# An attention, dense and routed-expert kernel: turns of the searches, halves for two copies, a bank for two logit tiles, and a number moved

## The chip, the cores and the metric

The kernel runs on one core of a Trainium2 chip. The metric is the device time of one execution in microseconds (us); the time of a kernel is the median of its runs. TensorE (PE) multiplies matrices, VectorE (DVE), ScalarE (ACT) and GpSimd (POOL) work on elements, SyncE (SP) and the others issue transfers (DMA). PSUM is the memory, in banks of 512 fp32 columns, into which PE writes; SBUF is the working memory.

## What is computed

Three stages follow each other: a linear attention with random features, a dense two-layer network, and eight experts to which 2304 tokens are assigned greedily, at most 288 tokens each, by order of their logits. The last stage, in which the change lies:

```python
logits = x @ w_gate                      # x: 2304 x 512, eight experts
order = np.argsort(-logits.flatten())
for idx in order:
    tok, e = idx // E, idx % E
    if assigned[tok] >= 0 or counts[e] >= cap:
        continue
    assigned[tok] = e
    counts[e] += 1
for e in range(E):
    h = np.maximum(x[assigned == e] @ w1[e], 0.0)
    out[assigned == e] = h @ w2[e]
```

## The kernel before

**Stages.** Attention runs to about 195 us, the dense network to about 609 us, the experts to the end. Products are made as three matmuls each (`mm3`, lines 203 to 206), of a high and a low part of both operands.

**The end of the dense network.** It works on five blocks: four of four tiles of 128 tokens, and one of the two tiles 16 and 17. `st_B` (L581) adds up the second layer in PSUM accumulators (tag `pj`). `st_x` (L546) copies each finished accumulator to SBUF (`xs`, L548), sends the rows to `xd` in DRAM (L550; tile 17 from ACT's queue, all others from SP's), and either notes eight dot products for DVE (`st_dot`, L562) or, for the tiles in `LT`, notes the tile for products on PE: `st_lT` (L565) transposes it (L569) and copies the transpose to SBUF (`xTt`, L571), `st_lg` (L574) multiplies it with the gate (L578) into the single bank of tag `tp` and reads eight logits out (L579). For tiles 16 and 17 this happens at the very end, in L641 to L643.

**The searches.** `finds` (L739) runs eight searches, numbered 0 to 7. Each finds the next expert that fills up, and its tokens. `begin` (L668) sets up keys from the logits `lg`. `closest` (L701) narrows a threshold in six iterations: DVE compares (`cmp`, L698), PE counts (L714), DVE tests (`ge`, L716), PE spreads the result (L719), DVE moves on (`dk` L723, `v2` L726). Then DVE marks the members (`so` L751, `sel` L754, `mem` L756 and L757), with `whose` (L786: L789, L791) writing the expert's number `e` between `so` and `sel`; PE counts places (`slots`, L800 and L801), and `numbers` (L811: `aa` L815 to L818, one-hots `OH` L832, their product L836) gives the token indices `idx` (L841). `outm` (L760) marks the tokens that stay. For searches 0, 1, 6 and 7 the numbers are finished in the search itself (yield `OH`); for 2 to 5 in the first two iterations of the following search (`fill`).

**The order of the work.** PE runs in the written order; the other engines' order is set by a planner from priorities and estimated readiness. Search 0 runs alone. When its indices are there, `fetch_x` (L855) gathers the expert's rows on POOL (L860), and a DVE instruction (L866) that waits for the last gather holds back the rest of the weights' loads on SP (`fetch_w`, L845). Meanwhile one step of search 1, and then `N1` more, go out (L989 to L991); then come the transposes of the gathered rows (`prep`, L879), and then the experts (`mlp`, L891). `mlp` gives control back after each turn of products, that is after one `mm3` of three matmuls, 64 times per expert; `visit` (L979) counts these turns down and takes the next step of the searches when `wait` runs out. How many turns lie between two steps is in `GAP` (L45), by the name of the step that the search has just yielded. So long as fewer than two searches are finished, L985 caps it at 3. From turn 57 of an expert on, the next expert's rows are transposed.

Of the kernel before, what the change touches and what calls it, by code (L numbers as in the profile page):

```python
# [20 lines left out]
def fused(tc, q, k, v, omega, w_in, w_out, w_gate, w1, w2, out):  # L21
# [22 lines left out]
    FZ, FS, PZ, PS = 6, 2, 56, 2  # L44
    HPF, RP, N1, GAP = 400, 30, 4, dict(cmp0=12, cmp5=3, cmp6=4, ge=2, mem=6, OH=7)  # L45
    DM = H * D
# [5 lines left out]
    with ctx:  # L52
# [493 lines left out]
        def st_x(t, acc):  # L546
            x = mb.tile([P, DM], F32, tag="xs", name="xs", bufs=XS)
            (nc.vector.tensor_copy if t % 2 and not 12 <= t < 16 else nc.scalar.copy)(x, acc)  # L548
            for rows, dst in x_rows(t):
                (nc.scalar if t == 17 else nc.sync).dma_start(dst, x[rows])  # L550
            if t in LT:
                xrow.append((t, x))
            else:

                dots.extend((acc if t >= 14 else x, lg[:, t, e:e + 1], e) for e in range(8))
# [3 lines left out]
        def st_dot(n):  # L559
# [3 lines left out]
            del dots[:n]  # L563

        def st_lT(x, copy):  # L565

            pt = ps("big")
            for c in range(4):
                nc.tensor.transpose(pt[:, c * P:(c + 1) * P], x[:, c * P:(c + 1) * P], ident)  # L569
            xT = mp.tile([P, DM], F32, tag="junk", name="xTt", bufs=2)  # L570
            copy(xT, pt)  # L571
            return xT

        def st_lg(t, xT):  # L574

            pg = ps("tp")
            for c in range(4):
                nc.tensor.matmul(pg[:, :8], xT[:, c * P:(c + 1) * P], wgn[:, c], start=c == 0, stop=c == 3, skip_group_check=True)  # L578
            nc.vector.tensor_scalar(lg[:, t], pg[:, :8], 0.0, None, ALU.add)  # L579

# [23 lines left out]
        def step(i):  # L604
# [28 lines left out]
            if i < len(steps):  # L633
                if t is not None:
                    st_lg(t, xT)
                st_dot(ND if i <= NB * NF else NE)
            elif i + 1 - LB == len(steps):
                st_dot(len(dots))
                nc.vector.tensor_scalar(lg[:, 0:12], lg[:, 0:12], 0.0, None, ALU.add)
                nc.vector.tensor_scalar(lg[:, 14:16], lg[:, 14:16], 0.0, None, ALU.add)  # L640
                xTs = [st_lT(x, copy) for (t, x), copy in zip(xrow, (nc.scalar.copy, nc.vector.tensor_copy))]  # L641
                for (t, x), xT in zip(xrow, xTs):
                    st_lg(t, xT)  # L643

# [94 lines left out]
        def finds():  # L739
# [3 lines left out]
            for k in range(E):  # L743
                res = rs[k]
                if k < E - 1:
# [5 lines left out]
                    nc.vector.tensor_tensor(so, st[0], e1b, ALU.mult)  # L751
                    whose(res, e1)
                    sel = small("sel", (P, NT))
                    nc.vector.tensor_reduce(sel, so, AX.X, ALU.max)  # L754
                    mem = small("mem", (P, 2, NT), BF)
                    nc.vector.scalar_tensor_tensor(mem[:, 0], vf, 0.0, sel, ALU.is_gt, ALU.mult)  # L756
                    nc.vector.scalar_tensor_tensor(mem[:, 1], vf, 0.0, sel, ALU.is_equal, ALU.mult)  # L757
                    q_ = yield from slots(mem.rearrange("p a t -> p (a t)"), 2)
                    out_ = small("outm", (P, NT))
                    nc.vector.tensor_scalar(out_, q_, GP + 0.5, None, ALU.is_gt)  # L760
                else:
# [6 lines left out]
                if k in (0, 1, E - 2, E - 1):  # L768
# [6 lines left out]
                    if k == 0:  # L775
                        yield "first"
                if k < E - 1:

                    nc.vector.scalar_tensor_tensor(lg, e1b, -3.0e38, lg, ALU.mult, ALU.add)
                    nc.vector.tensor_tensor(opn, opn, e1, ALU.subtract)  # L780

                    nc.vector.tensor_tensor(wt, wt, bc_e(out_), ALU.mult)
# [196 lines left out]
        def visit():  # L979
            wait[0] -= 1  # L980
            if wait[0] < 0:
                with tc.high_priority(offset=RP):
                    z = next(route, None)

                wait[0] = min(GAP.get(z, 0), 3) if found[0] < 2 else GAP.get(z, 0)  # L985

# [59 lines left out]
```

## Time and profile before

| | us |
|---|---|
| median of three runs (lowest to highest) | 958.03 (957.17 to 958.26) |
| the profiled execution, its own time | 955.96 |
| the profiled execution, its span from first to last instruction | 953.9 |

The span is 2.06 us shorter than the execution's own time, which is 2.07 us below the median. The mean granted TensorE clock is 0.962 of full speed. Times in rows count from the span's start. In rows of the order of time, the first two numbers are start and duration in us; `ACTq` and `SPq` are the DMA issues of an engine; a bracket at the end says how long the engine had been idle before the instruction, and what ended that.

### The profile page before, as it was taken

The numbers are of one execution on the slowest core, as the hardware profiler recorded it, in microseconds if no ns is written. First come the engines' busy times: TensorE is split into PE (matmuls) and PEld (weight loads), VectorE is DVE, ScalarE is ACT, GpSimd is POOL, SyncE is SP. The second block draws the span as 40 slices with busy tenths as digits, with TensorE's granted clock in tenths as the row PEclk, the third lists the DMA queues.
The fourth block names the chain that finished last, engine by engine and source line by source line (L and its number), as shares of the span: only waits on it lengthen the run. The fifth ranks groups of instructions, "written<-read, shape, count | busy, mean of one in ns | idle before, by whom it ended". The sixth has DMA issues, their size and how long they took to land. (4 is left out here: it accounts for less than half of the span.)

```text
span 953.9 us, 16517 instructions
## 1 busy us (share of the span) xinstructions
PE 877.3 (92%) x5923; PEld 770.3 (81%) x5923; DVE 630.1 (66%) x1645; ACT 483.9 (51%) x1062; POOL 476.3 (50%) x443
## 2 busy tenths in 40 slices
PE   7999799989999999999999999738998999998996
PEld 6998698968678888888888889628887888888996
DVE  4779889868877943882397256466774847866442
ACT  5777798955455355434534466303343343443552
POOL 6669756336664455445446446312443534436442
PEclk9999899999999999999999999858998989999999
DMA  8855532012311000100010010023641616428500
GB/s 209 222 158 168 133 111 68 23 67 67 108 70 44 1 1 1 45 0 1 1 45 1 0 45 2 23 69 133 202 165 62 203 45 208 154 74 256 197 26 25
DMA packets 74850, 81.90 MB, mean 86 GB/s; under 512 B 27016, under 2 KB 59784, under 8 KB 74640
## 3 DMA queue, kind: packets, MB, share of 16 engines
q1 hardware_dynamic: 71536, 71.15, 23.6%
q0 software_dynamic: 3072, 9.44, 3.2%
q8 instruction: 46, 0.75, 0.3%
q14 instruction: 36, 0.29, 0.1%
q10 hardware_dynamic: 160, 0.26, 0.1%
HBM read 71.39 MB, written 9.45 MB: 85 GB/s over the span
## 5 line engine op out<-in xcount | busy, mean ns | idle before, releaser
L905 POOL TENSOR_TENSOR iL<-We,iH 128x512 fp32r<-128x512 f32 x63 | 87.9, 1395 | 141.9 <-ACT iH L902 129.3
L496 POOL TENSOR_TENSOR iL<-W,iH 128x512 fp32r<-128x512 f32 x80 | 114.6, 1432 | 68.7 <-ACT iH L495 64.5
L204 PE MATMUL kv<-xH,iH 128*128 128x512 f32 (+2 forms) x372 | 130.3, 350 | 1.8 <-ACT xH L511 1.8
L206 PE MATMUL kv<-xH,iL 128*128 128x512 f32 (+2 forms) x372 | 127.7, 343 | 2.6 <-POOL iL L496 2.6
L205 PE MATMUL kv<-xL,iH 128*128 128x512 f32 (+2 forms) x372 | 127.9, 344 | 0.9 <-DVE xL L512 0.9
L504 POOL TENSOR_TENSOR oL<-W,oH 128x512 fp32r<-128x512 f32 x56 | 72.9, 1302 | 104.3 <-ACT oH L503 104.3
L206 PE MATMUL pj<-oH,gL 128*128 128x512 f32 x288 | 113.8, 395 | 0.0
L204 PE MATMUL pj<-oH,gH 128*128 128x512 f32 x288 | 113.7, 395 | 0.0
L205 PE MATMUL pj<-oL,gH 128*128 128x512 f32 x288 | 113.4, 394 | 0.0
L902 ACT CAST iH<-We 128x512 fp32r<-128x512 f32 x64 | 39.5, 619 | 113.8 <-PE kv L205 37.4
L269 ACT ACTIVATE kp<-pj,bias 128x128 f32<-128x128 f32 x288 | 79.1, 409 | 17.6 <-DVE bias L261 14.5
L562 DVE SCALAR_TENSOR_TENSOR junk<-xs,wgb 128x512 f32<-128x512 f32 x96 | 86.5, 948 | 0.0
L204 PE MATMUL pj<-hH,oH 128*128 128x288 f32 x256 | 84.1, 328 | 0.0
L206 PEld LDWEIGHTS kv<-xH,iL 128*128 128x128 f32 x372 | 71.6, 193 | 11.1 <-POOL iL L496 4.3
L204 PEld LDWEIGHTS kv<-xH,iH 128*128 128x128 f32 x372 | 71.4, 192 | 11.2 <-issue 3.0
L495 ACT CAST iH<-W 128x512 fp32r<-128x512 f32 x80 | 49.7, 621 | 59.1 <-PE kv L205 38.5
L205 PEld LDWEIGHTS kv<-xL,iH 128*128 128x128 f32 x372 | 71.6, 192 | 9.0 <-DVE xL L512 1.5
L205 PE MATMUL pj<-hL,oH 128*128 128x288 f32 x256 | 77.4, 302 | 0.6 <-DVE hL L927 0.5
L178 POOL TENSOR_TENSOR stg<-cg,stg 128x512 f32<-128x512 f32 x32 | 41.7, 1303 | 71.6 <-issue 30.4
L206 PE MATMUL pj<-hH,oL 128*128 128x288 f32 x256 | 76.9, 301 | 0.0
L532 DVE SCALAR_TENSOR_TENSOR kv<-r,kv 128x512 f32<-128x512 f32 (+1 forms) x53 | 34.0, 642 | 59.7 <-ACT r L531 59.6
L206 PE MATMUL s<-xH,iL 128*128 128x288 f32 (+2 forms) x204 | 68.6, 336 | 2.3 <-POOL iL L496 2.3
(377 smaller groups left out, 2262.0 us busy)
## 6 DMA issues: line engine op xcount, KB each, us to landing
We<-in_moe_w_dram SPq DMA_DIRECT2D x64, 512.0 KB, 4.5
stg<-in_moe_w_in_dram SPq DMA_DIRECT2D x16, 512.0 KB, 5.2
stg<-in_moe_w_out_dram SPq DMA_DIRECT2D x16, 512.0 KB, 3.5
ld<-in_k_dram SPq DMA_DIRECT2D x8, 512.0 KB
vf<-in_v_dram SPq DMA_DIRECT2D x32, 128.0 KB, 3.1
ld<-in_q_dram SPq DMA_DIRECT2D x8, 512.0 KB, 4.9
xd<-xs SPq DMA_DIRECT2D x16, 256.0 KB, 2.2
wgb<-wgd SPq DMA_DIRECT2D x1, 2048.0 KB
```

What stands on the lines that cost most here:

```text
L178: nc.gpsimd.tensor_tensor(lf, g.bitcast(F32), lf, ALU.mult)
L204: nc.tensor.matmul(o, aH, bH, start=first, stop=False, skip_group_check=True)
L205: nc.tensor.matmul(o, aH, bL, start=False, stop=False, skip_group_check=True)
L206: nc.tensor.matmul(o, aL, bH, start=False, stop=last, skip_group_check=True)
L269: nc.scalar.activation(kp[:, i, j], pjs[s // 4][:, s % 4], AF.Exp, bias=bias[:, i, j:j + 1])
L495: nc.scalar.copy(iH, wi)
L496: on_pool.append(nc.gpsimd.tensor_tensor(iL, wi, iH.bitcast(F32), ALU.subtract).ins)
L504: (nc.gpsimd if (ib > 0 if ib < NB else f % 2 == 0) else nc.vector).tensor_tensor(oL, wo, oH.bitcast(F32), ALU.subtract)
L532: nc.vector.scalar_tensor_tensor(ph[:, :n], r[:, :n], 1.0, ph[:, :n], ALU.min, ALU.mult)
L562: nc.vector.scalar_tensor_tensor(junk, x, 1.0, wgb[:, e], ALU.mult, ALU.mult, accum_out=d)
L902: nc.scalar.copy(iH, wi)
L905: (nc.vector if first and f == 0 else nc.gpsimd).tensor_tensor(iL, wi, iH.bitcast(F32), ALU.subtract)
```

## The change

- **Turns.** `N1` goes from 4 to 3; in `GAP`, `cmp5` goes from 3 to 4, `cmp6` from 4 to 5, `ge` from 2 to 1. While fewer than two searches are finished, every gap but that of `ge` is two smaller than in `GAP`, in place of the cap at 3.
- **Halves.** The accumulators of tiles 16 and 17, and their transposes, are each copied half by ACT and half by DVE (`both`).
- **One bank.** The logits of tiles 16 and 17 are made side by side in one PSUM bank and read by one instruction.
- **The number and `outm`.** `whose` stands behind the marks; `outm` stands behind the part of `numbers` that belongs to the search.

```diff
--- before.py
+++ after.py
@@ -42,7 +42,7 @@
 
     W1C, W2C, Z0 = 4, 4, 2
     FZ, FS, PZ, PS = 6, 2, 56, 2
-    HPF, RP, N1, GAP = 400, 30, 4, dict(cmp0=12, cmp5=3, cmp6=4, ge=2, mem=6, OH=7)
+    HPF, RP, N1, GAP = 400, 30, 3, dict(cmp0=12, cmp5=4, cmp6=5, ge=1, mem=6, OH=7)
     DM = H * D
     DFF = w_in.shape[1]
     N = B * S
@@ -545,7 +545,10 @@
 
         def st_x(t, acc):
             x = mb.tile([P, DM], F32, tag="xs", name="xs", bufs=XS)
-            (nc.vector.tensor_copy if t % 2 and not 12 <= t < 16 else nc.scalar.copy)(x, acc)
+            if t < 16:
+                (nc.vector.tensor_copy if t % 2 and t < 12 else nc.scalar.copy)(x, acc)
+            else:
+                both(x, acc)
             for rows, dst in x_rows(t):
                 (nc.scalar if t == 17 else nc.sync).dma_start(dst, x[rows])
             if t in LT:
@@ -561,6 +564,10 @@
                 junk = mp.tile([P, DM], F32, tag="junk", name="junk", bufs=2)
                 nc.vector.scalar_tensor_tensor(junk, x, 1.0, wgb[:, e], ALU.mult, ALU.mult, accum_out=d)
             del dots[:n]
+
+        def both(y, x):
+            nc.scalar.copy(y[:, 0:256], x[:, 0:256])
+            nc.vector.tensor_copy(y[:, 256:512], x[:, 256:512])
 
         def st_lT(x, copy):
 
@@ -571,12 +578,14 @@
             copy(xT, pt)
             return xT
 
-        def st_lg(t, xT):
+        def st_lg(t, xTs):
 
             pg = ps("tp")
-            for c in range(4):
-                nc.tensor.matmul(pg[:, :8], xT[:, c * P:(c + 1) * P], wgn[:, c], start=c == 0, stop=c == 3, skip_group_check=True)
-            nc.vector.tensor_scalar(lg[:, t], pg[:, :8], 0.0, None, ALU.add)
+            for j, xT in enumerate(xTs):
+                for c in range(4):
+                    nc.tensor.matmul(pg[:, 8 * j:8 * j + 8], xT[:, c * P:(c + 1) * P], wgn[:, c], start=c == 0, stop=c == 3,
+                                     skip_group_check=True)
+            nc.vector.tensor_scalar(lg[:, t:t + len(xTs)].rearrange("p t e -> p (t e)"), pg[:, :8 * len(xTs)], 0.0, None, ALU.add)
 
         def st_B(i):
             ib, f = steps[i]
@@ -632,15 +641,13 @@
                 st_B(i - LB)
             if i < len(steps):
                 if t is not None:
-                    st_lg(t, xT)
+                    st_lg(t, [xT])
                 st_dot(ND if i <= NB * NF else NE)
             elif i + 1 - LB == len(steps):
                 st_dot(len(dots))
                 nc.vector.tensor_scalar(lg[:, 0:12], lg[:, 0:12], 0.0, None, ALU.add)
                 nc.vector.tensor_scalar(lg[:, 14:16], lg[:, 14:16], 0.0, None, ALU.add)
-                xTs = [st_lT(x, copy) for (t, x), copy in zip(xrow, (nc.scalar.copy, nc.vector.tensor_copy))]
-                for (t, x), xT in zip(xrow, xTs):
-                    st_lg(t, xT)
+                st_lg(16, [st_lT(x, both) for t, x in xrow])
 
         i = 0
         with tc.manual_schedule(engines={ET.DVE, ET.Pool, ET.PE, ET.Activation}):
@@ -749,15 +756,13 @@
                     e1b = e1.unsqueeze(1).to_broadcast([P, NT, E])
                     so = small("so", (P, NT, E))
                     nc.vector.tensor_tensor(so, st[0], e1b, ALU.mult)
-                    whose(res, e1)
                     sel = small("sel", (P, NT))
                     nc.vector.tensor_reduce(sel, so, AX.X, ALU.max)
                     mem = small("mem", (P, 2, NT), BF)
                     nc.vector.scalar_tensor_tensor(mem[:, 0], vf, 0.0, sel, ALU.is_gt, ALU.mult)
                     nc.vector.scalar_tensor_tensor(mem[:, 1], vf, 0.0, sel, ALU.is_equal, ALU.mult)
+                    whose(res, e1)
                     q_ = yield from slots(mem.rearrange("p a t -> p (a t)"), 2)
-                    out_ = small("outm", (P, NT))
-                    nc.vector.tensor_scalar(out_, q_, GP + 0.5, None, ALU.is_gt)
                 else:
 
                     whose(res, opn)
@@ -775,6 +780,8 @@
                     if k == 0:
                         yield "first"
                 if k < E - 1:
+                    out_ = small("outm", (P, NT))
+                    nc.vector.tensor_scalar(out_, q_, GP + 0.5, None, ALU.is_gt)
 
                     nc.vector.scalar_tensor_tensor(lg, e1b, -3.0e38, lg, ALU.mult, ALU.add)
                     nc.vector.tensor_tensor(opn, opn, e1, ALU.subtract)
@@ -982,7 +989,7 @@
                 with tc.high_priority(offset=RP):
                     z = next(route, None)
 
-                wait[0] = min(GAP.get(z, 0), 3) if found[0] < 2 else GAP.get(z, 0)
+                wait[0] = GAP.get(z, 0) - 2 * (found[0] < 2 and z != "ge")
 
         with tc.manual_schedule(engines={ET.PE}):
             with tc.issue_after(rs[0]["placed"].ins):
```

## Rows read from the trace of the kernel before

**Rows 1.** The page's first part: busy us (share of the span) xinstructions, by engine
```profile
PE 877.3 (92%) x5923; PEld 770.3 (81%) x5923; DVE 630.1 (66%) x1645; ACT 483.9 (51%) x1062; POOL 476.3 (50%) x443
```

**Rows 2.** Busy time by stretch, columns named in the first line
```profile
core 0: us, PE busy (x) PEld busy (x) DVE busy (x) ACT busy (x) POOL busy (x), PEclk, DMA share, GB/s
...
615.00:620.00 5.00, 1.58 (x38) 1.31 (x38) 3.32 (x20) 0.00 (x0) 1.58 (x17) 0.50 0.01 3
...
665.00:670.00 5.00, 2.77 (x21) 2.40 (x19) 4.97 (x31) 1.55 (x3) 0.81 (x2) 1.00 0.22 63
...
770.00:775.00 5.00, 5.00 (x31) 4.65 (x28) 2.30 (x8) 1.81 (x4) 0.00 (x0) 0.50 0.00 0
775.00:780.00 5.00, 5.00 (x46) 4.64 (x45) 2.91 (x9) 2.25 (x5) 0.72 (x1) 0.87 0.01 3
...
900.00:905.00 5.00, 5.00 (x39) 5.00 (x39) 1.68 (x4) 2.68 (x6) 2.35 (x2) 1.00 0.00 0
```

**Rows 3.** Waits of PE from 647 us on: total us, times, longest
```profile
PE kv L886 <- DMA xg<-xd,idx: 4.8, 5, 1.2
...
PE tp L714 <- DVE cmp L698: 3.4, 6, 1.1
PE tp L800 <- DVE mem L757: 3.0, 3, 1.7
PE tp L719 <- DVE ge L716: 1.3, 3, 0.7
```

**Rows 4.** Order of time: tiles 16 and 17, and a half-size cast
```profile
598.80 0.37 ACT L533 CAST gH<-kv 128x256 fp32r<-128x256 f32 x1
...
608.82 0.59 ACT L548 COPY xs<-pj 128x512 f32<-128x512 f32 x1 [2.08 <-PE pj L206]
...
609.52 0.69 DVE L548 COPY xs<-pj 128x512 f32<-128x512 f32 x1 [2.33 <-PE pj L206]
...
610.25 1.24 ACTq L550 DMA_DIRECT2D xd<-xs  x2
...
612.11 1.63 PE L578 MATMUL tp<-wgn,xTt 128*128 128x8 f32 x8 [0.26 <-DVE lg L579]
...
613.98 0.17 DVE L579 TENSOR_SCALAR lg<-tp 128x8 f32<-128x8 f32 x1
```

**Rows 5.** Order of time: ACT and DVE at tile 14's accumulator
```profile
563.92 0.61 ACT L548 COPY xs<-pj 128x512 f32<-128x512 f32 x1
...
564.07 0.42 DVE L534 TENSOR_TENSOR gL<-s,gH 128x256 fp32r<-128x256 f32 x1 [0.90 <-ACT gH L533]
564.56 0.69 DVE L562 SCALAR_TENSOR_TENSOR junk<-pj,wgb 128x512 f32<-128x512 f32 x1
```

**Rows 6.** Order of time on DVE: marks of search 0
```profile
630.47 0.31 DVE L751 TENSOR_TENSOR so<-oh,e 128x144 f32<-128x144 bf16 x1
...
630.82 0.30 DVE L754 TENSOR_REDUCE sel<-so 128x18 f32<-128x144 f32 x1
...
632.43 0.18 DVE L760 TENSOR_SCALAR outm<-q__6676 128x18 f32<-128x18 f32 x1
632.52 0.17 DVE L815 TENSOR_SCALAR aa<-q__6676 128x18 f32<-128x18 f32 x1
```

**Rows 7.** Order of time on PE: the last steps ahead of the first expert
```profile
643.49 0.64 PE L714 MATMUL tp<-oh,cmp 128*32 128x8 bf16 x18 [1.76 <-DVE cmp L698]
...
644.80 0.55 PE L886 MATMUL kv<-ident,xg 96*128 96x96 f32 x2 [0.26 <-issue]
...
646.97 0.61 PE L204 MATMUL kv<-xH,iH 128*128 128x288 f32 x1
```

**Rows 8.** Order of time on PE: marks and one-hots of search 1
```profile
667.62 0.18 PE L800 MATMUL tp<-mem,ta 128*128 128x36 bf16 x1 [1.74 <-DVE mem L757]
...
670.75 1.08 PE L836 MATMUL tp<-mv,OH 128*96 128x6 bf16 x18 [1.23 <-DVE OH L832]
```

**Rows 9.** Order of time on PE: two waits of searches 2 and 3
```profile
681.42 0.61 PE L714 MATMUL tp<-oh,cmp 128*32 128x8 bf16 x18 [0.49 <-DVE cmp L698]
...
714.09 0.16 PE L719 MATMUL tp<-ge,onesu 32*128 32x8 bf16 x1 [0.68 <-DVE ge L716]
```

## The prediction

> **What bounds the kernel now.** I read the page's busy times first, then the busy time by stretch, then the waits of PE, then the instructions in order of time at the four places that the diff touches. TensorE is busy 92% of the span [rows 1], so what can be won is idle time of PE, and time at its lower clock. Both lie behind 609 us. From 615 to 620 us PE works 1.6 of 5 us, at half clock: the first search runs with nothing beside it, and DVE, PE and POOL hand a chain on until the first expert starts at 647 us [rows 2]. Behind that, PE works in its written order: expert products, and between them the small products of the next searches. One turn of products (three matmuls, after which the kernel looks whether a search step is due) takes 5.00 / 39 x 3 = 0.385 us at full clock, by the stretch 900 to 905 us [rows 2]. PE's waits behind 647 us are few and have names [rows 3]: 4.8 us on gathered rows, 3.4 us on comparisons, 3.0 us on marks, 1.3 us on `ge`, and further ones on one-hot tiles. In such a place DVE is full: 4.97 of 5 us between 665 and 670 us [rows 2]. The time of the whole is thus an entry chain of about 37 us, plus PE's work, plus these waits (12.5 us in the four rows) and what the half clock costs.
>
> **Copies in halves, logits in one bank.** Now tile 16 is copied by ACT at 608.82 us in 0.59 us, tile 17 by DVE from 609.52 to 610.21; the second group of logit products waits until DVE has emptied the bank of the first, runs 1.63 us from 612.11 (part of it at half clock), and its result is read at 613.98 [rows 4]. A half tile costs ACT 0.37 [rows 4] and DVE 0.42 us [rows 5] (a 128x256 cast and a subtraction that read PSUM, nearest in shape). If both halves run at once, tile 17 is ready at 609.95, each later copy ends 0.16 to 0.26 us sooner, the second group needs no emptied bank and runs mostly at full clock: read at about 612.85, 1.1 us won. If the halves of one bank go in turn, a copy takes 0.37 + 0.05 + 0.42 = 0.84 us, 0.25 and 0.15 us more than now. Then tile 17 is whole at 610.36, its transposes end near 611.0; ACT's queue also holds tile 17's two DMA issues, 1.24 us together [rows 4], which become ready before that transposed tile and sit ahead of its ACT half until 611.6; ACT and DVE halves end at 612.0 and 612.5, and the products at 613.0 to 613.4. That is still 0.3 to 0.7 us won, because the emptying in between is gone. If those DMA issues also come ahead of tile 16's transposed half, 0.3 us is lost. Which of the two it is, the nearest row says: DVE's first reading of tile 14's accumulator starts at 564.56 us, 0.03 us after ACT's copy of the same bank ended (563.92 + 0.61), though DVE had been free from 564.49 (564.07 + 0.42) [rows 5]: that looks like one engine at a time. I take 0.4 us won, between -0.3 and 1.1.
>
> The Trainium skill, "PSUM — Partial Sum Buffer", section "PSUM bank collisions raise a hardware error", speaks against this part: two engines on one bank and the same partitions at once, even two reads, are an error that software keeps apart by a dependency. By that rule the halves go in turn and the part is worth 0.4 us; without it, 1.1 us. The two rows agree with it, but are one case.
>
> **Expert's number behind the marks; `outm` later.** In search 0, `sel` (L754) starts at 630.82, 0.04 us after its input `so` (630.47 + 0.31) is done: the number's instruction at L789 fits into the latency in front of it [rows 6], so moving it wins nothing there. It makes `e`, and SP's load of the first expert's weights, some 0.4 us later. Nothing else is queued on SP then; the cover is the gather, for that load goes out about when L760 runs, at 632.4 [rows 6], and the first product starts only at 646.97 us [rows 7]. If that cover were gone it would cost these 0.4 us. `outm` (L760) stands in front of the `aa` of L815 by 0.09 us [rows 6]; moved behind the one-hots it runs under the gather: 0.1 us won. In later searches DVE has no gaps, and the three small instructions delay `mem` by 0 to 0.3 us; see below.
>
> **N1 from 4 to 3.** Before the first expert, PE's order holds L714, L719, L714, L719 of search 1 and then the transposes of the gathered rows. The last L714 ends at 643.49 + 0.64 = 644.13 us, the transposes start at 644.80 [rows 7]. With the last L719 moved behind the first turn of products they start about 0.6 us sooner (0.4 to 0.7: a semaphore wait may remain). Its follow-up on DVE (`dk`, `v2`, comparison) moves behind the expert's first splits, where three turns at half clock hide it. 0.6 us won, on the chain.
>
> **GAP, search 1.** I counted the turns by hand from the two formulas. The marks' product L800 comes at turn 28 (was 29), its `mem` is asked for at turn 23 (was 25), the one-hots' product L836 at 34 (was 33). So five turns instead of four lie in front of L800, which now waits 1.74 us, and six instead of four in front of L836, which waits 1.23 [rows 8]: 0.38 + 0.77 us, and 0.2 for the number's instructions, 1.35 at most. Against it, comparison 3 gets three turns instead of four, which may cost up to 0.55; and DVE, full there, may stretch. I take 0.8, between 0 and 1.4.
>
> **GAP, searches 2 to 6.** A comparison gets one turn more before its product, `ge` one less; an iteration keeps its seven or eight turns, except the first, so that a search takes 59 instead of 60. Where DVE is late, the wait only moves from L714 to L719 and nothing is won. Where only the comparison is late it is: 0.38 of the 0.49 us at 681.42 us [rows 9]. The other two waits on marks are 3.0 - 1.74 = 1.26 us together [rows 3]; with the number behind them I take 0.2 off each. Sum 0.8, between 0.2 and 1.0. The one-hots' product that frees the gather of expert 2 comes at turn 115 instead of 116, of expert 3 at 174 instead of 176, the gathered rows are wanted at 121 and 185 as before. At most 0.38 + 0.77 = 1.15 us of the 4.8 us on gathers goes; but `ge` stood late at just that place (0.68 us at 714.09 us [rows 9]) and eats about half: 0.6, between 0 and 1.1.
>
> **Sum.** 0.4 + 0.1 + 0.6 + 0.8 + 0.8 + 0.6 = 3.3 us off the profiled execution, whose span is 953.9 us and whose own time is 955.96: 950.6 and 952.7. The median of the runs shown is 958.03, 2.07 above that execution; so I forecast 954.7 for a median. The ends give 0.4 to 5.4 won, 957.6 to 952.6.
>
> **Rivals.** *A spared clock drop* (0.20): behind the wait on expert 3's rows the clock is 0.50 from 770 to 775 us and 0.87 in the next stretch [rows 2]: 5 + 1.3 us at half clock cost 3.15 us. If the shorter wait keeps the clock up, 954.7 - 3.15 = 951.5. For it: this wait shrinks most, by two turns. Against: the neighbours' waits remain, and drops may come up elsewhere. *Only the entry wins* (0.24): the searches are bound by DVE, the waits move from L714 to L719 one for one, and 0.4 + 0.1 + 0.6 = 1.1 us stays: 956.9. For it: 4.97 of 5 us on DVE. *Slower, by `ge`* (0.14): in the first two iterations of searches 2 to 6, where DVE also makes the older search's numbers, `ge` is queued behind them, and PE stands at L719, in order, with all later products behind it, one turn longer, while the comparison's extra turn pays nothing because DVE was not late there: 10 x 0.385 = 3.85 us lost, 1.1 won at the entry: 960.8. It decides once the waits at L719 grow from 1.3 to over about 3 us and those at L714 stay. Against it: only 3 waits on `ge` exist behind 647 us now.
>
> **How the numbers follow.** The forecast holds 0.42, the rivals 0.20, 0.24 and 0.14. The likeliest time is 954.7. Eight in ten reach from 951.0, just below the spared drop, to 959.5; beyond lie most of the slower case and the better ends of the spared drop. A measurement of this kernel tells about 0.2%, 1.9 us, from no change. Faster than 956.1: most of the forecast, the spared drop and a little of the entry case, 0.60. Slower than 959.9: 0.13. Between: 0.27.
>
> **What would show it.** Right: the last logit read 0.3 to 0.7 us sooner after the last product, with DVE's half behind ACT's; the first expert product about 1.1 us sooner than 646.97; L800 and L836 of search 1 waiting under 2.2 us together; L719 waits below 2.5 us. Wrong: halves that run beside each other, ACT's halves behind the DMA issues of both tiles, L719 waits above 3 us, or a clock that stays up from 770 to 780 us.

## The result and the profile after

The changed kernel takes 946.46 us (median of 7 runs, 945.88 to 947.95) where the kernel before takes 958.03; the ratio, estimated from all runs of both and not the quotient of the medians, is 0.9893, with a 95% interval from 0.9873 to 0.9912. It is faster by 11.6 us in medians and by 10.2 us by the ratio; the forecast was 3.3 us, 954.7, and the time lies below its range. In the table below, one slow run of e15 (1671 us) is left out. The profiled execution of after has a span of 943.9 us and a time of 946.46, against 953.9 and 955.96. In the changed kernel the lines from about 569 on are 7 higher: L714 is now L721 (`cmp`), L719 is L726 (`ge`), L800 is L807 (`mem`), L836 is L843 (`OH`), L886 is L893 (gathered rows).

First the page's busy times of after, against [rows 1]: the engines do nearly the same work; of PE's 2.9 us less, some 1.5 are the shorter time at half clock, below.

```profile
PE 874.4 (93%) x5923; PEld 768.3 (81%) x5923; DVE 634.6 (67%) x1646; ACT 485.0 (51%) x1064; POOL 475.2 (50%) x443
```

Then PE's waits of after from 646 us on (total us, times, longest), against [rows 3]:

```profile
PE tp L726 <- DVE ge L723: 2.4, 5, 0.6
PE kv L893 <- DMA xg<-xd,idx: 2.4, 3, 0.9
PE pj L205 <- DVE hL L934: 1.7, 2, 0.9
PE tp L721 <- DVE cmp L705: 1.4, 3, 0.8
PE tp L721 <- DVE oh L694: 1.1, 2, 0.6
PE tp L843 <- DVE dk L730: 1.0, 4, 0.3
PE tp L807 <- DVE mem L763: 1.0, 3, 0.6
PE tp L843 <- DVE OH L839: 0.5, 1, 0.5
```

Three lines of before that [rows 3] leaves out:

```profile
PE tp L836 <- DVE OH L832: 4.2, 3, 2.1
...
PE tp L714 <- DVE oh L687: 0.6, 1, 0.6
PE pj L205 <- DVE hL L927: 0.5, 1, 0.5
```

Gathered rows are down from 4.8 to 2.4 us, `cmp` from 3.4 to 1.4, `mem` from 3.0 to 1.0, the one-hots from 4.2 to 0.5; `ge` is up from 1.3 to 2.4, `hL` from 0.5 to 1.7, `oh` from 0.6 to 1.1. Next the entry in order of time, against [rows 4] and [rows 7]:

```profile
608.89 0.37 ACT L569 COPY xs<-pj 128x256 f32<-128x256 f32 x1 [2.08 <-PE pj L206]
609.30 0.42 DVE L570 COPY xs<-pj 128x256 f32<-128x256 f32 x1 [2.03 <-ACT xs L569]
...
612.27 1.07 PE L586 MATMUL tp<-wgn,xTt 128*128 128x8 f32 x8 [0.53 <-ACT xTt L569]
...
613.47 0.17 DVE L588 TENSOR_SCALAR lg<-tp 128x16 f32<-128x16 f32 x1 [0.79 <-PE tp L586]
...
643.59 0.64 PE L721 MATMUL tp<-oh,cmp 128*32 128x8 bf16 x18 [2.43 <-DVE cmp L705]
644.16 1.22 PE L893 MATMUL kv<-ident,xg 96*128 96x96 f32 x6
...
646.37 0.61 PE L204 MATMUL kv<-xH,iH 128*128 128x288 f32 x1
```

The last logit is read 0.51 us sooner (613.47 against 613.98), the first expert product starts 0.60 us sooner (646.37 against 646.97). So of the 10.0 us between the two spans, 0.6 come from the entry, and 9.4 from the stretch between the first expert product and the last transposes of results, which shrinks from 298.5 to 289.1 us.

I took that stretch apart in the same way for every run below: **length** from the first expert product to the end of the last transposes, **idle**, the sum of the gaps between PE's instructions in it, **rows**, the part of idle in front of the transposes of gathered rows, and **half clock**, the time in it in which the granted clock was 0.5 of full speed, the lower of its two levels (a stretch with a clock between counts by its share; by 0.5 us windows of busy time). Half clock costs half its length. Before: 298.5, idle 19.2, half clock 23.5. After: 289.1, 11.5, 20.6. So 7.7 of the 9.4 us are waits and some 1.5 are clock; what is left, 0.2, shows in neither. By experts' stages (the first from the first product, the others from the first transposes of that expert's rows, each to those of the next), the gain is in the first (37.0 to 34.9 us), the fourth (43.6 to 37.6, with the waits on expert 3's rows) and the sixth (37.3 to 32.0, with the waits on the last one-hots); the third and the fifth lost 2.5 and 2.1.

### The profile page after: what moved, and what is told of

It reads as the page before. It is cut to its first block, busy times and chain, and to the rows that moved or that the text cites. A ratio compares the mean times of both kernels' runs of the same rounds, so it can differ in the third digit from the quotient of the medians.

```text
span 943.9 us, 16523 instructions
## 1 busy us (share of the span) xinstructions
PE 874.4 (93%) x5923; PEld 768.3 (81%) x5923; DVE 634.6 (67%) x1646; ACT 485.0 (51%) x1064; POOL 475.2 (50%) x443
## 5 line engine op out<-in xcount | busy, mean ns | idle before, releaser
L912 POOL TENSOR_TENSOR iL<-We,iH 128x512 fp32r<-128x512 f32 x63 | 84.2, 1339 | 133.0 <-ACT iH L909 125.4
L269 ACT ACTIVATE kp<-pj,bias 128x128 f32<-128x128 f32 x288 | 79.4, 411 | 17.9 <-DVE bias L261 14.5
```

Source lines behind the costliest of these rows:

```text
L269: nc.scalar.activation(kp[:, i, j], pjs[s // 4][:, s % 4], AF.Exp, bias=bias[:, i, j:j + 1])
L912: (nc.vector if first and f == 0 else nc.gpsimd).tensor_tensor(iL, wi, iH.bitcast(F32), ALU.subtract)
```

## The experiments

Times are medians; the ratio is that to the kernel before, run beside it on the same chip, with its 95% interval. The last four columns are of the profiled execution.

| kernel | turns a search | us | ratio | length | idle | rows | half clock |
|---|---|---|---|---|---|---|---|
| before | 60 | 958.0 | 1 | 298.5 | 19.2 | 4.8 | 23.5 |
| e9 | 61 | 959.7 | 1.0029 [1.0010, 1.0047] | 299.1 | 19.9 | 6.9 | 24.1 |
| e5 | 59 | 949.3 | 0.9921 [0.9904, 0.9937] | 291.8 | 16.2 | 2.1 | 14.4 |
| e10 | 58 | 962.1 | 1.0049 [1.0028, 1.0069] | 305.1 | 22.8 | 1.6 | 34.0 |
| e2, tail | 60 | 956.5 | 0.9996 [0.9979, 1.0014] | 300.2 | 19.5 | 4.8 | 26.5 |
| e3, marks | 60 | 956.4 | 0.9993 [0.9977, 1.0009] | 298.6 | 19.3 | 4.9 | 24.0 |
| e6, exchange | 60 | 956.2 | 0.9991 [0.9972, 1.0010] | 300.1 | 17.6 | 3.9 | 31.5 |
| e8, search 6 sooner | 60 | 954.9 | 0.9979 [0.9964, 0.9993] | 297.8 | 17.7 | 4.7 | 27.1 |
| e1, all turns | 59 | 951.1 | 0.9931 [0.9907, 0.9955] | 288.6 | 14.1 | 2.4 | 13.4 |
| e4, later turns | 59 | 952.0 | 0.9934 [0.9913, 0.9956] | 294.5 | 16.6 | 0.9 | 21.4 |
| e7, turns and marks | 59 | 949.1 | 0.9907 [0.9883, 0.9931] | 291.4 | 14.9 | 3.0 | 17.6 |
| after | 59 | 946.5 | 0.9893 [0.9873, 0.9912] | 289.1 | 11.5 | 2.4 | 20.6 |
| e11, after, search 6 later | 59 | 947.8 | 0.9901 [0.9875, 0.9928] | 291.0 | 13.2 | 2.5 | 20.6 |
| e16, after | 60 | 957.4 | 1.0010 [0.9993, 1.0027] | 299.1 | 18.0 | 5.4 | 30.9 |
| e12, after | 58 | 960.5 | 1.0038 [1.0018, 1.0058] | 301.4 | 20.2 | 1.0 | 27.4 |
| e13, before, half splits | 60 | 955.0 | 0.9967 [0.9945, 0.9989] | 297.0 | 17.6 | 5.1 | 23.0 |
| e15, e10, half splits | 58 | 951.5 | 0.9944 [0.9924, 0.9964] | 295.3 | 17.0 | 2.1 | 23.6 |
| e14, after, half splits | 59 | 944.8 | 0.9883 [0.9859, 0.9908] | 286.1 | 11.7 | 3.2 | 14.0 |
| e17, before, no splits on POOL | 60 | 940.4 | 0.9830 [0.9805, 0.9855] | 283.3 | 8.6 | 5.4 | 20.0 |
| e18, e10, no splits on POOL | 58 | 935.1 | 0.9781 [0.9758, 0.9804] | 277.1 | 5.7 | 2.0 | 12.7 |

### The parts of the change by themselves

e1 is the kernel before with the three edits of turns alone (`N1`, `GAP`, the `wait` of `visit`); e2 has `both` and the one bank alone; e3 has `whose` and `outm` moved alone; e4 has the new turns only from the third search on, with `N1` 4.

```
e4:  wait[0] = dict(cmp0=3, cmp5=3, cmp6=3, ge=2, mem=3, OH=3).get(z, 0) if found[0] < 2 else GAP.get(z, 0)
     N1, GAP = 4, dict(cmp0=12, cmp5=4, cmp6=5, ge=1, mem=6, OH=7)
```

> The kernel before with the changed turns alone (N1, GAP, the formula); copies, logits and marks as before. Theory A, the turns: they take away nearly all of the 7.7 us of PE idle time that are gone behind the first expert's first product; the entry gains under 0.4 us. Expected 949.5 us (947.5 to 951.5) where the kernel before has 958.0. Theory B, a sum of small shifts: what is gone hangs on where the searches of the last experts fall against POOL's splits, so that any part moves it; then this run lies anywhere from 950 to 957 and the parts don't add up. Theory C, the marks: the turns alone give 3 us at most, 955.

> The kernel before with the copies in halves and the logits in one bank alone. Theory A: the last logits are read 0.5 us sooner, nothing else moves: 957.5 (956.5 to 958.0), with the idle time of PE behind the first expert's first product between 18 and 20.5 us. Theory B: a shift of 0.5 us of the whole entry changes later waits by 2 us or more either way. Theory C as A.

> The kernel before with the expert's number behind the marks and outm behind the numbers alone. Theory A: 0.1 us at the entry and 0.2 us at each of three waits on marks: 957.4 (956.5 to 958.0); the last search still waits about 2 us at its one-hots' product. Theory C, the marks: DVE's chain from the marks to the one-hots is what is freed in every search; then this run alone gives 4 us or more, below 954.5, and the waits on one-hots (4.2 us) fall below 2.

> The kernel before with the new turns only from the time on when two searches are finished (cmp5 4, cmp6 5, ge 1), and N1 and all gaps of search 1 as before. Theory A in its finer form: the idle time that went lies mostly in the stretches of experts 3 and 5 (2.7 and 2.9 of 7.7 us), so this run keeps about 6 us of the gain: 952 (950.5 to 954). If search 1's turns matter more (its waits fell by 1.2 us, and the clock came back 3.2 us sooner), it keeps 4 us or less: above 954.

The turns win 5.8 us by themselves (951.09 against 956.87 of the kernel before, run beside it; the profiled execution of e1, 945.21, was its fastest, so its last four columns flatter it). Tail and marks by themselves are not told apart from no change. By the ratios the three parts add up to 0.80%, the whole change to 1.07%; the intervals are too wide to say whether the parts help each other. With `N1` and search 1's turns as before (e4) it is 951.99: these two are worth less than the runs tell apart, though each shows in the trace (below; the later searches of e4 also stand one turn sooner than those of e1, for search 1 is a turn shorter there). What can be measured of the gain is in the turns of the searches from the third on.

### Which property of the turns

The new numbers do two things: they give `cmp` a turn more and `ge` a turn less, and they make a search 59 turns long instead of 60. e5 has only the second, e6 only the first. Counted in the traces, the searches of e5 stand one turn sooner than those of the changed kernel (its one-hots' products come at turns 114, 173 and 232, against 115, 174 and 233 there and 116, 176 and 236 before), since search 1 is as before in it. e7 is the change without its tail. e8 is the kernel before with its last search alone four turns sooner.

```
e5:  GAP = dict(cmp0=11, cmp5=3, cmp6=4, ge=2, mem=6, OH=7)                          (before: cmp0=12)
e6:  e4's two lines with cmp0=13
e8:  wait[0] = min(GAP.get(z, 0), 3) if found[0] < 2 else GAP.get(z, 0)
    +wait[0] -= 4 * (z == "cmp0" and found[0] == 5)
```

> The kernel before with one number changed: cmp0 from 12 to 11, so that each search from the third on takes 59 turns instead of 60, as in the changed kernel, while cmp5, cmp6 and ge keep their old turns. Theory D, the drift: what wins is that later searches, and with them the gathers of experts 2 and 3 and the one-hots of the last two searches, come one to four turns sooner against the experts' products. Then this run keeps what the late turns alone kept: 952 (950.5 to 953.5), with no wait on expert 3's rows above 1 us and less than 0.5 us on the last one-hots. Theory E, the exchange: what wins is the comparison's extra turn at the price of ge's; then this run stays at 956 to 958.

> The kernel before with the new turns of cmp5, cmp6 and ge from the time on when two searches are finished, and cmp0 raised from 12 to 13, so that a search keeps its 60 turns: the exchange without the drift. Theory D: 956 to 958.5, with waits on expert 3's rows (1.7 us) and on the last one-hots (2 us or more) as before. Theory E: 952 (950.5 to 953.5).

> The changed kernel with the copies and logits of tiles 16 and 17 as before: turns and marks together. The turns alone took 951.1 and the changed kernel 946.5. If turns and marks help each other (the changed kernel waits 0.55 us on ge at search 5's first iteration where the turns alone wait 1.83 us), this run is near the changed kernel: 947.2 (946 to 948.5). If it is the copies that move the entry against the clock's fall, it stays near 951.

> The kernel before with search 6 alone begun four turns sooner, so that searches 6 and 7 stand at the turns that the changed kernel gives them, and all else as before. Theory D: the waits on the last two one-hots (0.9 and 2.1 us) fall under 0.5 us together and the half-clock stretch behind them goes: 3 to 4.5 us faster, 953 (951.5 to 954.5). If the place against the products doesn't matter: 956 to 958, with those waits still there.

One number, `cmp0` 11 for 12, wins 7.8 us; the exchange of `cmp` and `ge` wins nothing that can be measured. That one turn adds up from search to search: in the changed kernel the one-hots' product for expert 3's rows comes two turns sooner, the last one four. Of the 6.7 us that e5's length loses, 2.6 are waits on rows and some 4.5 half clock, which is 9.1 us shorter; the other waits are 14.1 us against 14.5, for the two on the last one-hots are gone and others have come. Two lines of e5's waits:

```profile
PE kv L886 <- DMA xg<-xd,idx: 2.1, 2, 1.1
...
PE tp L836 <- DVE OH L832: 1.2, 1, 1.2
```

e7 lies between its two cases, and its interval overlaps those of e1 and of after: it decides nothing. e8 takes the two waits on the last one-hots away (the sixth stage goes from 37.3 to 31.7 us, idle 0.06), but a wait of 1.85 us comes up at 830 us, on the one-hots `oh` with which the last search starts, and 2.2 us are left of the gain:

```profile
829.22 1.49 POOL L905 TENSOR_TENSOR iL<-We,iH 128x512 fp32r<-128x512 f32 x1 [1.66 <-ACT iH L902]
...
829.49 1.38 DVE L676 TENSOR_TENSOR w__9811<-w__9811,ta 128x144 f32<-128x144 f32 x1
...
832.02 0.62 PE L714 MATMUL tp<-oh,cmp 128*32 128x8 bf16 x18 [1.85 <-DVE oh L687]
```

L676 makes an input of `oh` and takes 0.3 us elsewhere; I saw what stands beside it only later (below).

After these I held that a search that stands sooner has more margin: rows and one-hots come before PE wants them. The next four were to show that.

### The margin holds for the rows alone

```
e9:  cmp0=13, e10: cmp0=10            (in the kernel before)
e12: cmp0=11                          (in the changed kernel; 58 turns there)
e11: +wait[0] += 4 * (z == "cmp0" and found[0] == 5)      (in the changed kernel)
```

> The kernel before with one turn more between two searches (cmp0 13: a search takes 61 turns, not 60). Theory of the margin (a search that is k turns later against the products lets PE wait k turns longer for gathered rows and for the last one-hots, and the clock falls behind such waits): the waits on expert 2's and 3's rows and on the last one-hots, which are there already, grow by 1 to 6 turns of 0.385 us each, idle time of PE from the first product on rises from 18 to 21 us or more, and the time is 3 to 6 us above that of the kernel before. Rival (the gain of 59 turns was a lucky place of a few waits and clock drops): within 2 us of the kernel before, idle time 17 to 19 us.

> The kernel before with two turns less between two searches (cmp0 10: 58 turns). With 59 turns it gained 7.8 us. Theory of the margin: the waits on rows and last one-hots are gone already with 59, so a further turn wins at most 1 to 2 us and may lose as much on comparisons, since each search stands closer behind the numbers of the one before: 947 to 952. Rival (every turn sooner counts the same): 941 to 943.

> The changed kernel with its last search alone held back by four turns, so that its one-hots come where they came before. Theory of the margin: two waits on the last one-hots near 865 and 872 us come back, 2 to 3 us together, and a stretch of half clock behind them: 948.5 to 951, with the last stages as in the kernel before. Rival (the stage before expert 7's rows is won by another part of the change): no wait there, within 1 us of the changed kernel's 946.5.

> The changed kernel with one turn less between two searches (cmp0 11: 58 turns, not 59). Theory of the margin: the changed kernel still waits 2.4 us on gathered rows and 1.1 us on oh in three to five places; a turn sooner takes 0.4 to 1 us of these, and comparisons may eat it: 945 to 948. Rival (each turn sooner wins some 7 us as it did in the kernel before): 939 to 941.

For the gathered rows the theory holds: their waits are 6.9, 4.8, 2.1 and 1.6 us with 61, 60, 59 and 58 turns, and 2.4 and 1.0 in the changed kernel with 59 and 58. For the whole it falls. A turn more than 60 costs 2.7 us, less than expected, since the waits on the last one-hots shrink to 0.09 and 0.67; and a turn less than 59 loses 12.8 us in the kernel before (949.3 to 962.1) and 14.0 in the changed one (946.5 to 960.5). With 58 turns the searches are sooner everywhere, and yet the waits on the last one-hots are back, longer than with 60 (2.69 and 1.02 us in e10), and there are others on `cmp`, `ge` and `oh`, of 2.4, 1.7 and 1.7 us. The rival that each turn sooner wins as much again falls too. e11 has one of the two waits back, 2.2 us at 865 us, and half clock behind it; its 1.3 us over the changed kernel are less than the two intervals tell apart.

What these waits have in common shows in the order of time on DVE and POOL. The kernel before, ahead of its last one-hots:

```profile
869.76 1.85 DVE L815 TENSOR_SCALAR aa<-sl 128x18 f32<-128x18 f32 x1
870.28 1.29 POOL L905 TENSOR_TENSOR iL<-We,iH 128x512 fp32r<-128x512 f32 x1
...
871.86 1.45 POOL L905 TENSOR_TENSOR iL<-We,iH 128x512 fp32r<-128x512 f32 x1 [0.29 <-ACT iH L902]
...
872.11 1.27 DVE L822 TENSOR_TENSOR jj<-aa 128x54 f32<-128x54 f32 x1
...
874.26 1.08 PE L836 MATMUL tp<-mv,OH 128*96 128x6 bf16 x18 [2.06 <-DVE OH L832]
```

L815 takes 0.17 us elsewhere [rows 6]; here it takes 1.85 and ends at 871.61, 0.04 us behind POOL's split of the expert's weights (870.28 + 1.29). L822, 0.22 us elsewhere, is held by the next split likewise. These two holds, 2.7 us together, cover what PE waits, 2.06 us. The same place in the changed kernel:

```profile
861.37 0.18 DVE L822 TENSOR_SCALAR aa<-sl 128x18 f32<-128x18 f32 x1
...
862.57 1.12 DVE L839 TENSOR_TENSOR OH<-tb,q 128x864 bf16<-128x864 bf16 x2
...
863.61 3.21 DVE L916 TENSOR_TENSOR oL<-We,oH 128x256 fp32r<-128x256 f32 x1
863.99 2.53 POOL L912 TENSOR_TENSOR iL<-We,iH 128x512 fp32r<-128x512 f32 x2
864.00 0.93 PE L843 MATMUL tp<-mv,OH 128*96 128x6 bf16 x18
```

Here the search's steps run while POOL issues gathers, and the one-hots' product goes without a wait; the hold falls on `oL`, a split for a product that comes later. With 58 turns (e10) the hold is on the one-hots themselves:

```profile
876.05 2.19 DVE L832 TENSOR_TENSOR OH<-tb,q 128x864 bf16<-128x864 bf16 x2
876.09 1.68 POOL L905 TENSOR_TENSOR iL<-We,iH 128x512 fp32r<-128x512 f32 x1 [1.15 <-ACT iH L902]
876.71 0.56 PE L836 MATMUL tp<-mv,OH 128*96 128x6 bf16 x9 [2.69 <-DVE OH L832]
```

Over the whole stretch I compared each DVE instruction with the lower quartile of its own line, tile and shape. In the kernel before, 18 last over 0.8 us longer than that, in the changed kernel 19, and each of them lies beside one of POOL's splits; instructions that lie beside none sum to 2 to 3 us of excess. The sum beside splits is not what differs (22.2 us before, 26.7 after), and its part on steps of the searches differs little (20.6 before, 19.4 after): which step is hit, with how much slack, sets the wait. That is a theory so far; it predicts that shorter holds, with all turns left alone, bring 58 turns back.

### Shorter holds, and none

In e13 to e15 POOL's split is cut in two; the order of the instructions of PE and ACT stays the same to the last one in the traces, and so does that of DVE but for swaps of neighbours in a few places of e13 and e14. e16 is the changed kernel with 60 turns. In e17 and e18 the splits on POOL are left out, a tile of zeros stands for their results, and PE makes the same products in the same order (some neighbours on DVE change places).

```
e13, e14, e15:
-   (nc.vector if first and f == 0 else nc.gpsimd).tensor_tensor(iL, wi, iH.bitcast(F32), ALU.subtract)
+   for c in [slice(0, 4)] if first and f == 0 else [slice(z, z + 2) for z in range(0, 4, 2)]: (nc.vector if first and f == 0 else nc.gpsimd).tensor_tensor(iL[:, c], wi[:, c], iH[:, c].bitcast(F32), ALU.subtract)
e16: cmp0=13 in the changed kernel
e17, e18:
+   zL = rp.tile([P, 4, P], F32R, tag="zL", name="zL", bufs=1)              (once, ahead of the experts)
+   nc.gpsimd.memset(zL.bitcast(F32), 0.0)
...
-   iL = rp.tile([P, 4, P], F32R, tag="iL", name="iL", bufs=2)
+   iL = rp.tile([P, 4, P], F32R, tag="iL", name="iL", bufs=1) if first and f == 0 else zL
...
-   (nc.vector if first and f == 0 else nc.gpsimd).tensor_tensor(iL, wi, iH.bitcast(F32), ALU.subtract)
+   if first and f == 0:
+       nc.vector.tensor_tensor(iL, wi, iH.bitcast(F32), ALU.subtract)
```

> The kernel before, with the splits of the weights that POOL makes (iL, 128x512 in about 1.3 us) cut into two instructions of 128x256; the order of all engines is otherwise as before, to the last instruction, and so are the turns. Theory of the collisions (a DVE instruction of a search that falls beside one of POOL's splits is held until that split ends; which one is hit decides the waits): a hit holds 0.65 us instead of 1.3 to 1.85, the two waits on the last one-hots (0.90 and 2.06 us) fall below 1.5 us together, idle time of PE behind the first product falls from 18 to 15 us, and the time to 951 to 955. Rival (what counts is the turn at which a step is asked for): the turns are the same, so 956 to 958, with the same waits.

> The changed kernel with POOL's splits in halves likewise. Theory of the collisions: its hits fall mostly on oL, which has slack, so little is left: 944 to 946.5. Rival (turns): 946 to 947.5. If shorter splits slow POOL down as a whole: above 948.

> The kernel before with 58 turns a search, which took 962.1 us and waited 2.7, 2.4 and 1.7 us in places where it waited little with 60, and with POOL's splits in halves. Theory of the collisions: those long waits fall to about half, 953 to 958. Rival (58 turns are too few for the comparisons by themselves): 960 to 963.

> The changed kernel with one turn more between two searches, so that a search takes 60 turns as before, while all its other parts stay (halves, one bank, marks, N1, the turns of search 1, cmp and ge exchanged). If the place of the later searches against the experts carries the gain: 952 to 956, with other waits and clock drops in the stages of experts 2 to 5. If the other parts carry it: 947 to 949.

> The kernel before without POOL's splits of the experts' first weights: the low parts iL are left out (one constant tile of zeros stands for them), all products are still made, so that PE has the same work in the same turns (60 a search) and POOL keeps only its gathers and scatters. Theory of the collisions: no DVE instruction is held by over 0.8 us, waits on the one-hots of the last search (0.90 and 2.06 us) go below 0.7, idle time behind the first product from 18 to 10 to 14 us; 943 to 951. Rival (the waits come from the turns and from DVE's load alone): waits as before, 954 to 958.

> The same (POOL's low parts left out) with 58 turns a search, which with the splits cost 5 us over 60 turns. Theory of the collisions: without them 58 and 60 turns stand within 3 us of each other, both under 951. Rival (58 turns are too few in themselves): still 4 to 6 us above the run with 60 turns.

With 58 turns the halves win 10.6 us (962.1 to 951.5, each run beside its own runs of the kernel before), with nothing else changed: POOL's splits, not the number of turns, made 58 slow. The waits on the one-hots fall from 5.0 to 1.2 us; the longest wait on `cmp`, 2.4 us, stays, again behind four halves of POOL in a row (834.57 to 837.84 us). With 60 they win 2.3 us, and the wait on the last one-hots stays, against what I expected. Its cause is in the order of time of e13:

```profile
868.92 3.35 DVE L815 TENSOR_SCALAR aa<-sl 128x18 f32<-128x18 f32 x1
869.43 2.80 POOL L905 TENSOR_TENSOR iL<-We,iH 128x256 fp32r<-128x256 f32 x4
...
873.85 0.81 PE L836 MATMUL tp<-mv,OH 128*96 128x6 bf16 x12 [2.48 <-DVE OH L832]
```

POOL has fallen behind through its gathers and has four halves ready in a row; DVE comes in only after the fourth. In the changed kernel the halves give 944.8 us, the least of the kernels that leave nothing out, but its interval overlaps that of after.

Without POOL's splits, DVE has no instruction left that lasts even 0.2 us over its quartile, the kernel before falls by 16.1 us (956.5 to 940.4), and the order of 58 and 60 turns is reversed: 58 is 5.2 us faster, more than the 3 us that I had allowed between them. PE's waits with 60 turns (e17):

```profile
PE kv L888 <- DMA xg<-xd,idx: 5.4, 5, 1.7
PE tp L836 <- DVE OH L832: 1.2, 1, 1.2
PE tp L836 <- DVE dk L723: 1.0, 4, 0.3
PE tp L800 <- DVE mem L757: 0.9, 1, 0.9
```

and with 58 (e18):

```profile
PE kv L888 <- DMA xg<-xd,idx: 2.0, 2, 1.1
PE tp L836 <- DVE dk L723: 1.4, 4, 0.6
PE tp L836 <- DVE OH L832: 1.2, 1, 1.2
PE tp L800 <- DVE mem L757: 0.9, 1, 0.9
```

The waits on `cmp` (but for 0.2 us in e18) and on the last one-hots are gone in both, so POOL's splits made them. That products with zeros are faster explains little of the 16.1 us: the last two experts, with no search beside them, take 28.0 and 28.4 us from their first products on before, and 27.9 and 28.4 in e17, 0.1 us less each at most. Of the 15.2 us that e17's length loses, 10.6 are waits and 1.8 clock; some 2 more show in neither and are not explained. What two turns less still win there is 3.3 us of waits on gathered rows and 7.3 us of half clock. Only 3.4 of these 7.3 stand behind the waits on expert 3's rows; another 3.4 stand behind search 1's one-hots, where both kernels wait the same 1.23 us, so that 1.7 us cannot be put down to the turns. The margin is thus some 1.8 to 2.6 us a turn, which the holds more than cover in e10. How much of the 7.8 us between 60 and 59 turns (e5) is margin and how much holds that fell elsewhere was not measured, as 59 turns were not run without POOL's splits; if the margin is as large there, 5 to 6 are left for the holds and the clock behind them.

e16 shows whose gain it is. With 60 turns and all its other parts, the changed kernel is at 957.4, the same as the kernel before (957.29, run beside it). Its searches from the third on stand a turn later than before, at turns 117 and 177 where the kernel before has 116 and 176, because search 1 is a turn longer; so a turn's worth of margin is lost in it as well. Its first two lines of PE's waits:

```profile
PE tp L726 <- DVE ge L723: 7.0, 5, 1.8
PE kv L893 <- DMA xg<-xd,idx: 5.4, 6, 1.4
```

## Why the prediction was wrong in size

**What bounds the kernel** was right: PE's work stayed, and 7.7 us of waits and 2.9 us of half clock went.

**Halves and one bank**: right. DVE's half starts at 609.30, when ACT's (608.89 + 0.37) is done, as [rows 5] had it. The trace agrees with the rule that I weighed there (the Trainium skill, "PSUM — Partial Sum Buffer", section "PSUM bank collisions raise a hardware error": software has to keep two engines apart that read the same partitions of one bank), with 0.04 us between the two. ACT's DMA issues come ahead of its half of tile 17's transposed copy; the products run 612.27 to 613.34, inside the 613.0 to 613.4 of the working. Read 0.51 us sooner, and 0.6 counted from the start of the copy; forecast 0.4, between 0.3 and 0.7 for halves in turn. By itself (e2) that can't be measured.

**Number and `outm`**: right at the entry; by themselves (e3) no difference.

**N1**: right by itself, wrong in the sum. The transposes start 0.64 us sooner (644.16 against 644.80), as forecast. But I added the tail's 0.4 and `outm`'s 0.1 to it, and these were gone by then: the counting product ahead of the transposes starts at 643.59, 0.10 us later than in [rows 7], though the logits were read 0.51 sooner, because it waited longer on `cmp` (2.43 against 1.76). The rows of DVE show why, before and after:

```profile
641.96 0.26 DVE L726 SCALAR_TENSOR_TENSOR v__6812<-v__6774,dk,dg 128x36 bf16<-128x36 bf16 x1
642.91 0.15 DVE L866 SCALAR_TENSOR_TENSOR e<-xg,ei 1x1 int32<-1x1 int32 x1 [0.69 <-DMA xg<-xd,idx]
```

```profile
641.20 0.17 DVE L730 TENSOR_REDUCE dk<-tp 128x1 f32<-128x8 f32 x1 [0.25 <-PE tp L726]
642.73 0.15 DVE L873 SCALAR_TENSOR_TENSOR e<-xg,ei 1x1 int32<-1x1 int32 x1 [1.36 <-DMA xg<-xd,idx]
642.81 0.24 DVE L733 SCALAR_TENSOR_TENSOR v__6814<-v__6776,dk,dg 128x36 bf16<-128x36 bf16 x1
```

`dk` is still 0.56 us sooner (641.20 against 641.76), but DVE's next instruction in the chain, `v2` (L733), now stands behind the one that waits for the last gather (L873), in front of which it stood before; that gather landed only about 0.2 us sooner, and DVE idles 1.36 us for it. The first product came 0.60 us sooner, not 1.1.

**Search 1**: right in mechanism, low in size. L807 and L843 wait 0.60 and 0.45 us where L800 and L836 waited 1.74 and 1.23 [rows 8], under the 2.2 that I named; a `cmp` wait of 0.77 came up at 660 us, a little over the 0.55 that I had allowed for. The first stage shrank by 2.1 us in place of 0.8: 1.4 of waits, and half clock 2.9 us shorter, which I hadn't counted. In the seven kernels with the new `N1` and turns of search 1 the granted clock rises to 1.0 at 3.1 to 4.0 us behind the first product, in the thirteen without at 5.9 to 7.8 us, but for e9 (3.6).

**Searches 2 to 6, and the gathers of experts 2 and 3**: this is the step that failed. I had counted that a search takes 59 turns instead of 60 and priced it at 0.6 us, with the gathers of experts 2 and 3 alone; it won 7.8 (e5). Four things are wrong in it. The waits on rows fell by 2.6 us (e5; 2.4 in after), where I had capped them at 1.15: those on expert 3's rows, 1.66 us, went altogether in both, though the two turns of the changed kernel are 0.77 us (e5 has three there); where the rest comes from is open. The turn adds up over the searches, and I followed it only to the third; the waits on the last one-hots, two of the "further ones on one-hot tiles" that I had left out of the sum, were 2.96 us with half clock behind them. I took a DVE instruction to last as long as in its usual row, though the trace of before shows L815 at 1.85 us and L822 at 1.27 ahead of one of these waits. And I took a turn sooner to be a gain that only `ge` could eat; e10 and e12 show that the next turn sooner loses all of it, because other steps fall beside POOL's splits. The exchange that got 0.8 of my sum was worth nothing (e6).

**The rivals.** *The spared clock drop* came in one sense. The busy time by stretch of after, against [rows 2]:

```profile
750.00:755.00 5.00, 4.40 (x36) 4.14 (x34) 4.32 (x19) 0.93 (x2) 1.35 (x1) 0.73 1.04 364
...
770.00:775.00 5.00, 5.00 (x52) 4.63 (x51) 4.32 (x12) 2.26 (x6) 1.32 (x1) 1.00 0.01 3
775.00:780.00 5.00, 5.00 (x52) 4.62 (x51) 2.37 (x10) 2.91 (x6) 3.72 (x4) 1.00 0.21 60
```

The clock stays up from 770 to 780 us, but falls between 750 and 763 us and again near 824, so that only 2.9 of 23.5 us of half clock went. I had said that drops may come up elsewhere. *Only the entry wins* is refuted by e1 and e5. *Slower by `ge`* didn't come, as the waits at L726 stayed at 2.4 us, under the 3 that I gave; but its mechanism is real: with 60 turns and the new `ge` (e16) they are 7.0 us, and the gain is gone.

## What to carry to other kernels

Where PE waits on a short chain of DVE instructions, look for links that last many times what the same line lasts elsewhere, and at what POOL does just then; a step priced from its usual row is priced too low beside a POOL split. The waits on rows fell with every turn, but the whole had no slope: 61, 60, 59 and 58 turns gave 959.7, 957, 949.3 and 962.1 us. A shift that wins is to be tried with its neighbours, and a forecast for it needs a range that holds both signs. To see what lies beneath, leave out the work that collides and compare again: without POOL's splits the shift from 60 to 58 turns, which had cost 5 us, won 5.2.

## What the runs showed of the hardware

A DVE instruction of 0.17 us lasted 1.85 us beside a POOL instruction of 1.29 us, and 3.35 us beside four in a row that took 2.80 us together: DVE did not come in between them. The Trainium skill, "SBUF — State Buffer", section "SBUF: two separate sides", says that DVE and GpSimd share a pair of ports, that the one that starts first holds it for its whole instruction and the other blocks; of DVE's instructions it names those with two SBUF inputs and those in a 2-port mode. The rows agree in that the held instruction ends 0.04 us behind POOL's; whether L815, with one input, ran in such a mode no row shows. That DVE waited through four POOL instructions in a row is what e13 adds. In both cases L815 starts some 0.5 us ahead of the first split's recorded start, while POOL still issues a gather; why the hold begins so soon is open.

The stretch ahead of the experts is the same program in all these kernels up to 608 us, yet tile 16's transposes start between 608.2 and 611.8 us in their profiled executions. A part of a change that is worth half a microsecond can't be read from one execution's span, only from the distance between two rows of it.
